# Seven products for eight in the v projection of three layer-1 chunks

## The chip, the cores and the metric

The kernel runs on one core of one Trainium2 chip. The metric is device time in microseconds, the median of several executions of the same program. A core has five engines that run side by side and wait for each other by semaphores: TensorE (matrix products), VectorE and ScalarE (elementwise work), GpSimd (small work and some transfers) and SyncE (which issues most transfers). TensorE writes its results to PSUM, eight banks of 128 x 512 float32; the others copy them from there to SBUF. In the profile they are called PE, DVE, ACT, POOL and SP.

## The reference, cut to what matters

Two layers of attention and gated feed-forward, each with a residual and a normalization in front. The same weights serve both layers.

```python
def _A_ref(x, wqkv, wo):            # x: 1 x 2048 x 1024, wqkv: 1024 x 3072
    qkv = (x @ wqkv) ...            # split into q, k, v of 32 heads of 32
    # token s attends to s, s-2, ..., s-14 (8 keys), softmax, weighted sum of v
    return o @ wo
def _B_ref(x, w1, w3, w2):          # 1024 x 3584, 1024 x 3584, 3584 x 1024
    return (silu(x @ w1) * (x @ w3)) @ w2

x = x + _A_ref(_layernorm(x), A_wqkv, A_wo)
x = x + _B_ref(_layernorm(x), B_w1, B_w3, B_w2)
x = x + _A_ref(_layernorm(x), A_wqkv, A_wo)
x = x + _B_ref(_layernorm(x), B_w1, B_w3, B_w2)
```

The change touches one part: v, the last third of `x @ wqkv`, in the second layer.

## The kernel before

The 2048 tokens are cut in four chunks of 512. The program first computes q, k and v of layer 0 for all four chunks, 24 banks of 8 matmuls for each chunk (for chunk 0, q is done by another routine). Then come eight feed-forward stages, one for each layer and chunk; after the stages 1 to 4 (counted from 0) stands the q, k, v part of one layer-1 chunk. Attention runs on VectorE beside all of this, and its output projection is put in between, two tiles at a time.

From the third stage on, the feed-forward products use a scheme of seven products for eight: the operands are cut in 2 x 2 blocks, sums of blocks are formed, and seven block products (P1 to P7) replace eight. The sums of the weight blocks are made once, during the first two stages, scaled to fit float16, and stored in DRAM (`t_d`); an *early* tile holds the four blocks of P1, P2, P5, P6 and a *late* tile the three of P7, P3, P4. The sums of the activation blocks are four VectorE steps per stage (`norm_sums`), one of them in place.

The plain projection, used for q, k and v alike, writes one bank after the other:

```python
def q_part(l, c, which, ws, then=()):
    ready = ready_norm(("Q", l, c))
    ...
    for t0 in range(0, KT, SG):
        ...                                     # sgt: a slot in big (l = 0) or hT (l = 1)
        for t in range(t0, t0 + SG):
            ps = bank("ps")                     # six PSUM banks in rotation
            for kk in range(KT):
                nc.tensor.matmul(ps[:], lhsT=ws[kk // KH][:, kk % KH, t::KT], rhs=xnT[:, kk, :], ...)
            r = pe(KT, ready)
            background(r)
            nc.scalar.copy(sgt[:, t - t0, :], ps[:])
            ...
        nc.sync.dma_start(qkv_d[l][which][:, t0:t0 + SG, c * CH:(c + 1) * CH], sgt)
        between(False)                          # also puts waiting ScalarE work here
```

The pipeline of seven products works on groups of 256 output rows (two blocks of 128) by 512 tokens; a product is 2 x 4 matmuls of 256 columns. Its steps, cut to what waits for what:

```python
def head_part(i, name):
    if name == "P1":                 # A = P1; B = copy of A
        G["A"] = acc(); run(G, name, G["A"], True)
        G["B"] = acc(); nc.scalar.copy(G["B"][:], G["A"][:])
    elif name == "P5":               # D = P5; s5 = copy of D
        ...
    elif name == "P6":               # A += P6, so after the copy of A; su = copy of A; D += su
        run(G, name, G["A"], False, G["tB"])
        nc.scalar.copy(su, G["A"][:])
        background(t + 0.8)
        nc.vector.tensor_tensor(G["D"][:], G["D"][:], su, op=ALU.add)
    elif name == "P2":               # B += P2: quarter 0 is done
        ...
    elif name == "P7":               # A += P7; s22 = A + s5 on VectorE: quarter 3 is done
        run(G, name, G["A"], False, G["tU"])
        background(r + 0.8)
        if G["corner"]:
            s22 = G["corner"]()
            nc.vector.scalar_tensor_tensor(s22, G["A"][:], G["inv"], s5, op0=ALU.mult, op1=ALU.add)
        ...
    elif name == "P3":               # D += P3: quarter 1 is done
        run(G, name, G["D"], False, G["tD"])
    else:                            # P4: A += P4, after the VectorE step of P7: quarter 2 is done
        run(G, name, G["A"], False, G["tC"])

for i in range(n + 1):               # group i's first half is woven with group i-1's second half
    for name, tail in (("P1", "P7"), ("P5", "P3"), ("P6", "P4"), ("P2", None)):
        if i < n: head_part(i, name)
        if tail and i: head_part(i - 1, tail)
        if tail and i and fill and i == n and tail != "P4": fill(...)
    done(i)
```

(The `fill` puts matmuls of the next product, with w2, between the last P7, P3 and P4; the loop is shortened here.)

ScalarE's and VectorE's work that is not tied to a product waits in queues. The program is put in order when it is built, by clocks (`now`) that the builder keeps for each engine: an item is emitted when these clocks say that it fits. On ScalarE:

```python
gate = [2.2]
def act_background():
    for queue in (acts, sizes, parts, reads):
        while True:
            s = head(queue)
            if s is None or max(now["act"], s[1]) + s[0] > now["pe"] + gate[0]:
                break
            take_act(queue)
```

`acts` are the normalizations: for each half chunk four passes that measure two tiles, a short chain on GpSimd, then two passes that apply (`ACTIVATE xn<-x_sb,mom`), each followed by a DMA transpose to `xnT`. `sizes` measure w2, in squares of 128 x 2048 or 128 x 1536 elements with a sum; `parts` and `reads` measure w1 and w3 and make scaled copies.

The q, k, v part after a stage:

```python
b_stage(u, with_q)
if with_q:
    for which in range(3):
        if which == 2:
            between(False, True)
        q_part(*units[q], which, [weight("qkv"), weight("qkv")])
        release(2)
```

Of the kernel before, what the change touches and what calls it, by code (L numbers as in the profile page):

```python
# [7 lines left out]
FP32 = mybir.dt.float32  # L8
# [9 lines left out]
def kernel(  # L18
# [197 lines left out]
    down_scale = const.tile([P, 2, NG], FP32, name="down_scale")  # L216
    size2 = const.tile([P, 16], FP32, name="size2")
    total = const.tile([P, 1], FP32, name="total")
    down2 = const.tile([P, 1], FP32, name="down2")
    up2 = const.tile([P, 1], FP32, name="up2")  # L220
    peak = const.tile([P, 3], FP32, name="peak")
    hsum = const.tile([P, HTN // 2, HT], FP16, name="hsum")
    h16 = hT[:].bitcast(FP16)
    t2_d = [dram.tile([P, 7, (b - a) // 2, 512], FP16, name=f"t2_d{i}") for i, (a, b) in enumerate(fsplits)]
    t_d = [[dram.tile([P, 14, KT // 2, P], FP16, name=f"t_d{m}_{g}") for g in range(NG)] for m in range(2)]
    qkv_d = [[dram.tile([P, KT, S], BF16, name=f"qkv_d{l}_{i}") for i in range(3)] for l in range(2)]

# [72 lines left out]

    adds, acts, makes, reads, parts, sizes = [], [], [], [], [], []

# [52 lines left out]
    def take_act(queue):  # L355
        cost, ready, emit = queue[0][1]
        act(cost, ready)
        queue[0][1] = None
        emit()
# [3 lines left out]
    def act_background():  # L363
        for queue in (acts, sizes, parts, reads):
            while True:
                s = head(queue)
                if s is None or max(now["act"], s[1]) + s[0] > now["pe"] + gate[0]:
                    break
                take_act(queue)
# [309 lines left out]
    for u in range(len(units)):  # L679
# [14 lines left out]
        if 1 <= u and u + 3 < len(units):  # L694
            seq += [("qkv", which, h) for which in range(3) for h in range(2)]
    w_tiles, w_at, due, used = [], {}, [], [0]

    def load_weight(pieces=1):
# [25 lines left out]
        else:  # L724
# [4 lines left out]
            if rest[0]:  # L729
                got = {}  # L730
                parts.append([weight_size(*rest[0], w, at, got), None])
                reads.append([weight_sums(*rest[0], w, got), None])
        w_at[len(w_tiles)] = at
# [50 lines left out]
    def queue_q(q):  # L784
# [3 lines left out]
        queue_norm(key, units[q][1], range(R))  # L788
        

# [28 lines left out]

    def q_part(l, c, which, ws, then=()):  # L820

# [7 lines left out]
        for t0 in range(0, KT, SG):  # L829
            i = (c * 3 + which) * KT // SG + t0 // SG  # L830
            i = i % (7 if l == 0 else 8) * SG
            sgt = big[:, i * CH:(i + SG) * CH].bitcast(BF16).rearrange("p (a t) -> p a t", a=SG) if l == 0 else hT[:, i:i + SG, :]
# [16 lines left out]
            if l == 0:  # L849
                stored[:] = landed, landed  # L850
            if first and t0 == SG:
# [4 lines left out]
        qkv_at[l, c, which] = landed  # L856
        if which == 1:
            plain_left.discard(("Q", l, c))
        if which == 2:
            xnT_free["Q", l, c] = now["pe"]  # L860
# [54 lines left out]

    pending, stored, made, held = [0] * 2, [0.0] * 2, set(), []
    junk = hsum[:].bitcast(BF16).rearrange("p k t -> p (k t)")

    def differences(m, g, a, r):

        b = blocks[a]
        for out, x, y in ((4, 5, 1), (1, 1, 0), (2, 4, 0), (6, 3, 2)):
            yield 0.40, r, lambda: nc.vector.tensor_tensor(
                b[:, out], b[:, x], b[:, y], op=ALU.add if (x, y) == (4, 0) else ALU.subtract)
        pending[a] -= 1
        nc.gpsimd.dma_start(t_d[m][g][:, 4 * a:4 * (a + 1)], b[:, 0:4])
        nc.gpsimd.dma_start(t_d[m][g][:, 8 + 3 * a:8 + 3 * (a + 1)], b[:, 4:7])
        stored[a] = now["dve"] + 7.0

    def finish_sums(done):  # L930

        while not done():
            if head(reads) is not None:
                take_act(reads)
            elif head(parts) is not None:
                take_act(parts)
            elif head(makes) is not None:
                take(makes)
            else:
                pe_requests(1, True)  # L940
# [60 lines left out]
    def sums_of_w2(i, f, ws, loaded):  # L1001

        while "at" not in got2 or all(pending):
            yield "blocked"
# [30 lines left out]
    def pipeline(key, groups, consume, done, last, fill=None):  # L1035
# [66 lines left out]
        for i in range(n + 1):  # L1102
            for name, tail in (("P1", "P7"), ("P5", "P3"), ("P6", "P4"), ("P2", None)):
# [6 lines left out]
                if tail and i:  # L1110
# [5 lines left out]
                    if fill and i == n and tail != "P4":  # L1116
                        fill(int(tail == "P3"))
            done(i)

    def products(u, f0, f1, hold):  # L1120
# [132 lines left out]
    def b_stage(u, hold):  # L1253
# [5 lines left out]
        for (f0, f1) in fsplits:  # L1259
# [44 lines left out]
            for hh in range(2):  # L1304
                now["pe"] = max(now["pe"], *times[hh])
                for j in range(TPC):
# [10 lines left out]
                    if step == 0:  # L1317
                        steps = range(u * nq // 2, (u + 1) * nq // 2)
                        reads.extend([sums_of_w2(split, f, tiles, max(times[0] + times[1])), None] for f in steps)
                    act_background()  # L1320
# [27 lines left out]
    for c in range(NCH):  # L1348
        for which in range(3):
# [11 lines left out]
            if c >= 1:  # L1361
                then = (then + (None,) * 3)[:3] + (part_of_w2,)
            q_part(0, c, which, w_tiles[2 * which:2 * which + 2], then)
            if c == NCH - 1:
                release(2)
            if which == 0 and c == 1:
# [3 lines left out]
    for u, (l, c) in enumerate(units):  # L1370
# [6 lines left out]
        if with_q:  # L1377
            for which in range(3):
                if which == 2:
                    between(False, True)  # L1380
                q_part(*units[q], which, [weight("qkv"), weight("qkv")])
                release(2)


# [28 lines left out]
```

## Time and profile before

| | |
|---|---|
| time, median of 3 | 1532.38 us (1532.05 to 1533.98) |
| span of the profiled execution | 1531.0 us |
| layer 0: q, k, v of four chunks | to about 192 us |
| feed-forward stages 0 and 1, plain | about 192 to 514 us |
| q, k, v of layer-1 chunk 0 | 514.0 to 556.5 us |
| stages 2, 3, 4, by seven products | from 556.5, 742.8 and 927.1 us |
| q, k, v of layer-1 chunks 1, 2, 3 | 700.9 to 742.8, 885.2 to 927.1, 1072.6 to 1114.1 us |

The span is cut by where the lines of the kernel begin and end on TensorE in the chain that ended last. In the profile a row of groups gives the line, engine, operation, names and shapes, the count, then busy time and mean of one in ns, then idle time before it and what ended it. A row of the timeline gives start and duration in us first. A row of waits gives who waited for whom, the sum in us, the number of times, the longest. A row of the chain in order of time gives start, length and what it was. L836 is the plain projection, L1052 a product of the seven, L1165 one with w2, L840 the eviction of a projection bank, L345 the applying pass of a normalization, L958 a square of w2, L1064 the copy of P1's bank, L1073 that of P6, L1076 VectorE's sum after P6, L1088 and L1090 its sum after P7, L590 and L665 the multiplications of the attention, L771 the output projection.

### The profile page before, as it was taken

How to read it: one execution, taken by the hardware profiler on the slowest of the kernel's cores; microseconds unless marked ns; L12 is line 12 of the kernel's file. 1: busy time of each engine (PE TensorE's matmuls, PEld its weight loads, DVE VectorE, ACT ScalarE, POOL GpSimd, SP SyncE). 2: the span in 40 equal slices, each digit the busy share in tenths (PEclk: the TensorE clock that was granted, in tenths of full speed). 3: DMA queues.
4: the chain of work that ended last, by engine and by line, in shares of the span. 5: the costliest groups of instructions: out<-in, count | busy, mean ns of one | idle time of the engine just before them, and what ended most of it. 6: DMA issues, size and time to landing. Idle time of an engine off the chain costs nothing.

```text
span 1531.0 us, 25095 instructions
## 1 busy us (share of the span) xinstructions
PE 1518.1 (99%) x9594; PEld 989.5 (65%) x9634; DVE 1201.8 (78%) x2126; ACT 884.1 (58%) x1388; POOL 153.7 (10%) x308
## 2 busy tenths in 40 slices
PE   9999999999999999999999999999999999999999
PEld 7666644444444577575786767766677767686865
DVE  4688998889989898989698958898678986435445
ACT  3885476567665357455565564756557445554643
POOL 1210102121211101001011010100111000000000
PEclk9999999999999999999999999999999999999999
DMA  9777969798997888979779997898969988878885
GB/s 321 202 218 215 253 226 330 272 304 289 306 320 247 280 316 294 347 264 303 263 269 324 346 268 282 280 323 302 323 225 333 338 296 282 306 272 334 318 294 203
DMA packets 261432, 439.56 MB, mean 287 GB/s; under 512 B 73856, under 2 KB 201088, under 8 KB 245056
## 3 DMA queue, kind: packets, MB, share of 16 engines
q1 hardware_dynamic: 248464, 390.90, 76.8%
q0 software_dynamic: 12704, 46.93, 8.6%
q8 instruction: 75, 1.23, 0.3%
q14 instruction: 45, 0.37, 0.1%
q10 hardware_dynamic: 144, 0.13, 0.0%
HBM read 345.90 MB, written 67.90 MB: 270 GB/s over the span
## 4 chain that ended last, share of the span: by engine, by line
PE 97%; ACT 1%; issue 1%; DVE 0%; DMA 0%; SPq 0%; ACTq 0%
PE st L1052 32%; PE ps L836 21%; PE w L1165 16%; PE po L771 7%; PE pg L1279 6%; PE pu L1288 6%; PE acc L1310 6%; PE pq L444 1%; PE L L604 0%; DMA wqkv<-in_A_wqkv_dram 0%; ACT L629 0%; ACT L1227 0%; ACT E L629 0%; ACT sg L1227 0%; DVE x_sb L1150 0%
## 5 line engine op out<-in xcount | busy, mean ns | idle before, releaser
L836 PE MATMUL ps<-xnT,wqkv 128*128 128x512 f16 (+1 forms) x1469 | 320.4, 379 | 0.2
L1052 PEld LDWEIGHTS <-early 128*128 128x128 f16 x2688 | 262.6, 98 | 40.4 <-issue 3.5
L836 PEld LDWEIGHTS <-wqkv 128*128 128x128 bf16 x1472 | 210.6, 144 | 108.1 <-issue 2.2
L1165 PE MATMUL w<-t,hT 128*128 128x512 f16 x1008 | 226.0, 379 | 0.6 <-ACT big L1185 0.5
L1052 PEld LDWEIGHTS <-late 128*128 128x128 f16 x2016 | 197.2, 98 | 30.6 <-issue 2.5
L590 DVE TENSOR_TENSOR tree<-qT,kT 128x2048 bf16<-128x2048 bf16 x128 | 156.3, 1221 | 35.8 <-DMA kT<-qkv_d 18.2
L1052 PE MATMUL st<-xnT,late 128*128 128x256 f16 x1344 | 174.2, 273 | 2.2 <-ACT big L1073 2.2
L510 DVE TENSOR_TENSOR tree<-tree 128x1024 bf16<-128x1024 bf16 x256 | 175.6, 686 | 0.9
L1052 PE MATMUL st<-big,early 128*128 128x256 f16 x1344 | 172.3, 273 | 1.6 <-ACT sg L1227 1.1
L1165 PEld LDWEIGHTS <-hT 128*128 128x128 f16 x1008 | 98.2, 98 | 112.9 <-DVE hT L1136 2.0
L1052 PE MATMUL st<-xnT,early 128*128 128x256 f16 x1344 | 165.7, 273 | 0.0
L665 DVE TENSOR_TENSOR tree<-At,vT 128x2048 bf16<-128x2048 bf16 x128 | 156.2, 1221 | 11.9 <-DMA At<-E 10.7
L1064 ACT COPY st<-st 128x512 f32<-128x512 f32 x84 | 48.3, 575 | 128.1 <-PE st L1052 127.4
L771 PE MATMUL po<-wo,oT 128*128 128x512 bf16 x486 | 110.8, 379 | 1.3
L840 ACT CAST hT<-ps 128x512 bf16<-128x512 f32 x96 | 55.8, 585 | 90.6 <-PE ps L836 88.3
L1288 PE MATMUL pu<-xnT,w3t 128*128 128x512 f16 x448 | 105.8, 379 | 0.0
L1279 PE MATMUL pg<-xnT,w1t 128*128 128x512 f16 x448 | 105.8, 379 | 0.0
L1310 PE MATMUL acc<-w2t,hT 128*128 128x512 bf16 x437 | 97.8, 379 | 0.6
L1076 DVE TENSOR_TENSOR st<-st,big 128x512 f32<-128x512 f32 x84 | 58.4, 695 | 46.9 <-ACT big L1073 46.8
L1227 ACT ACTIVATE sg<-st,down_scale 128x512 bf16<-128x512 f32 x126 | 86.6, 687 | 11.6 <-PE st L1052 11.0
L1052 PE MATMUL st<-big,late 128*128 128x256 f16 x672 | 87.1, 273 | 0.0
L771 PEld LDWEIGHTS <-oT 128*128 128x128 bf16 x512 | 50.1, 98 | 55.7
(167 smaller groups left out, 1916.6 us busy)
## 6 DMA issues: line engine op xcount, KB each, us to landing
early<-t_d SPq DMA_DIRECT2D x84, 1024.0 KB, 6.9
late<-t_d SPq DMA_DIRECT2D x84, 768.0 KB, 6.2
t<-t_d SPq DMA_DIRECT2D x42, 1024.0 KB, 7.3
t<-t_d SPq DMA_DIRECT2D x42, 768.0 KB, 5.3
wqkv<-in_A_wqkv_dram SPq DMA_DIRECT2D x28, 1024.0 KB, 8.1
w1t<-in_B_w_dram SPq DMA_DIRECT2D x14, 1024.0 KB, 7.6
w3t<-in_B_w_dram SPq DMA_DIRECT2D x14, 1024.0 KB, 11.0
t_d<-big POOLq DMA_DIRECT2D x28, 512.0 KB, 6.2
```

What stands on the lines that cost most here:

```text
L510: nc.vector.tensor_tensor(b, b, buf[:, 4:8, :], op=ALU.add)
L590: V.tensor_tensor(pr, qT[:], kT[:, :, k0:k0 + TCH], op=ALU.mult)
L665: V.tensor_tensor(tm.rearrange("p w (a e) -> p w a e", a=4), At[:].rearrange("p a w e -> p w a e"), win, op=ALU.mult)
L771: nc.tensor.matmul(ps[:], lhsT=oT[:, t, j * P:(j + 1) * P], rhs=wo[:, t, hh * 512:(hh + 1) * 512], start=(t == 0), stop=(t == KT - 1))
L836: nc.tensor.matmul(ps[:], lhsT=ws[kk // KH][:, kk % KH, t::KT], rhs=xnT[:, kk, :], start=(kk == 0), stop=(kk == KT - 1))
L1052: nc.tensor.matmul(out[:, a, :], lhsT=w[:, a, blk, k, :], rhs=rhs[:, k, :], start=start and a == 0 and k == 0, stop=k == KQ - 1, skip_grou ...
L1076: nc.vector.tensor_tensor(G["D"][:], G["D"][:], su, op=ALU.add)
L1165: nc.tensor.matmul(out[:], lhsT=lhs[:, k, j * P:(j + 1) * P], rhs=w[:, k, :], start=start and k == 0, stop=k == nq - 1, skip_group_check=True)
L1227: nc.scalar.activation(sg[:], src, ACTF.Silu, scale=inv)
L1279: nc.tensor.matmul(pg[:], lhsT=w1t[:, kk, fi * P:(fi + 1) * P], rhs=xnT[:, kk, :], start=(kk == 0), stop=(kk == KT - 1))
L1288: nc.tensor.matmul(pu[:], lhsT=w3t[:, kk, fi * P:(fi + 1) * P], rhs=xnT[:, kk, :], start=(kk == 0), stop=(kk == KT - 1))
L1310: nc.tensor.matmul(acc[:], lhsT=hT[:, f, j * P:(j + 1) * P], rhs=tiles[hh][f // nq][:, f % nq, :], start=(f == 0), stop=(f == f1 - f0 - 1))
```

## The change

Seven products need fewer matmul columns than eight. The change uses them for v of the layer-1 chunks 1, 2 and 3; the q and k parts stay plain. The weights must be scaled and their block sums formed first, so:

- in layer 0, eight ScalarE passes square one eighth of v's weights each and sum the squares. They stand in a queue of their own, `lazy`, behind all the others.
- in the q, k, v part of layer-1 chunk 0 (after stage 1), v is done first, still plain; while v and q run, ScalarE makes 16 scaled copies of v's weight blocks, VectorE 16 differences, and they go to DRAM. The order there is v, q, k.
- for chunks 1, 2 and 3, q and k are plain, and then `v_products` runs a pipeline of two groups. The sums of the activation blocks for it are queued ahead of those for the next stage; the in-place one waits for k.

```diff
     def act_background():
-        for queue in (acts, sizes, parts, reads):
+        for queue in (acts, sizes, parts, reads, lazy):
...
+    def size_of_v(i, w, at):
+
+        for k in range(KH):
+            yield 1.10, at, lambda: nc.scalar.activation(junk[:, 0:D], w[:, k], ACTF.Square,
+                                                         accum_out=size_v[:, KH * i + k:KH * i + k + 1])
+        if i == 1:
+            total_scale(size_v, up_v, down_v, got_v)
+
+    def sums_of_v(ws, at):
...
+                for i, (kh, fh) in ((0, (0, 0)), (1, (0, 1)), (3, (1, 0)), (5, (1, 1))):
+                    t = 4 * g + 2 * fh + a
+                    yield 0.65, max(at, got_v["at"], stored[slot]), lambda: nc.scalar.activation(
+                        b[:, i], ws[kh][:, :, t::KT], ACTF.Copy, scale=up_v[:])
+                makes.append([differences(2, g, a, now["act"] + 0.1, slot), None])
+        made.add("v")
...
     def queue_q(q):
...
         queue_norm(key, units[q][1], range(R))
-        
+        if q > NCH:
+            adds.append([sum_later(key), None])
...
+    def v_products(l, c):
...
+        def consume(G, q, src, r):
+            pair, t0 = q % 2, HT * (q // 2)
+            to = stage(G, pair)
+            if q != 3:
+                nc.scalar.activation(to[:, :, t0:t0 + HT], src, ACTF.Copy, scale=down_v[:])
+                r = act(0.57, r)
...
+        groups = []
+        for g in range(2):
+            G = dict(m=2, g=g, inv=down_v[:])
+            G["corner"] = lambda G=G: stage(G, 1)[:, :, HT:CH]
+            groups.append(G)
+        pipeline(key, groups, consume, lambda i: between(False, i == 0), True)
+        xnT_free[key] = now["pe"]
...
+            if (c, which) == (1, 0):
+                for i in range(2):
+                    lazy.append([size_of_v(i, w_tiles[4 + i], 40.0), None])
             q_part(0, c, which, w_tiles[2 * which:2 * which + 2], then)
             if c == NCH - 1:
+                while which == 2 and head(lazy) is not None:
+                    take_act(lazy)
                 release(2)
...
         if with_q:
-            for which in range(3):
-                if which == 2:
-                    between(False, True)
-                q_part(*units[q], which, [weight("qkv"), weight("qkv")])
+            if u == 1:
+                for which in (2, 0, 1):
...
+                    q_part(*units[q], which, ws, (), 1, 4)
...
+                force(makes, lambda: not any(pending))
+                continue
+            for which in range(2):
+                q_part(*units[q], which, [weight("qkv"), weight("qkv")], (), 1)
                 release(2)
+            v_products(*units[q])
```

The change also orders some queues anew: `finish_sums`, which empties the weight copies at the end of a stage, now lets other VectorE work run in between, and the copies of w2 go ahead of copies of w1 and w3 that are not yet due.

## The prediction

> **What bounds the kernel now.** I read the page's busy shares first, then the chain that ended last, then that chain in order of time, then what TensorE waited for.
>
> ```profile
> PE 1518.1 (99%) x9594; PEld 989.5 (65%) x9634; DVE 1201.8 (78%) x2126; ACT 884.1 (58%) x1388; POOL 153.7 (10%) x308
> PE 97%; ACT 1%; issue 1%; DVE 0%; DMA 0%; SPq 0%; ACTq 0%
> ```
>
> TensorE is the chain: 97% of the span is matmul after matmul. A busy share alone would not prove it; the pace does. From the chain in order of time, one plain stretch and one stretch of seven products:
>
> ```profile
> 700.86 31.08 PE ps L836 x144
> 830.14 34.93 PE st L1052 x320
> ```
>
> 31.08/144 = 0.2158 us for a matmul of 512 columns, 34.93/320 = 0.1092 us for one of 256: nothing stands between them. The longest rows of what TensorE waited for, in the whole kernel:
>
> ```profile
> PE st L1052 <- ACT big L1073: 2.2, 1, 2.2
> PE pq L444 <- DMA wqkv<-in_A_wqkv_dram: 1.4, 2, 0.7
> PE pw L200 <- DVE tree L195: 1.2, 1, 1.2
> PE st L1052 <- ACT sg L1227: 1.1, 1, 1.1
> ...
> ```
>
> So what removes columns gains their full time, and what makes TensorE wait costs its full time. The first row is the only kind of wait that matters below: a product that accumulates onto a bank which ScalarE had not yet copied.
>
> [...] here its 273 ns for 256 columns overlap at a pitch of 109, so I count starts and not durations.
>
> **What is removed.** A plain v part is 8 banks x 8 matmuls x 0.2158 = 13.81 us. Seven products are 2 groups x 7 x 8 = 112 matmuls of 256 columns x 0.1092 = 12.23 us. The difference is 1.58 us, for three chunks 4.75 us, 0.3% of the time. That is the most there is to gain.
>
> **What is added and lies beside.** In layer 0: eight squares of 128x1024, 1.06 us plus 0.2 for the accumulator (the durations of the norms' squares), so 10 us of ScalarE in a stage of 24 banks per chunk, where its busy share is four to eight tenths. In the q, k, v part of the first layer-1 chunk: 16 scaled copies x 0.71 = 11.4 us of ScalarE and 16 differences x 0.42 = 6.8 us of VectorE, in 42 us in which ScalarE was busy for 15; and 3.5 MB of writes. By the order of the compiled program the copies end 12 evictions before this part does. None of it should hold TensorE. Weights for v grow from 2 to 3.5 MB per chunk; six tiles are loaded ahead, so I charge nothing.
>
> **What is added and lies on the path.** The pipeline of seven products has eight or six groups to fill it in the gate and up stages and two here, and after the last group nothing stands between P7, P3 and P4. I walked the three v parts with the durations of the old trace. Zero is the end of k's last bank. A product takes 8 x 0.1092 = 0.873. An engine starts about 0.2 after a product's last slot, as the old trace has it at the first copies of a stage. Rows of the timeline, then of the groups:
>
> ```profile
> 1097.34 1.24 ACT L345 ACTIVATE xn<-x_sb,mom 128x1024 f16<-128x1024 bf16 x1
> 1098.59 0.58 ACT L840 CAST hT<-ps 128x512 bf16<-128x512 f32 x1
> 1099.07 1.24 ACT L345 ACTIVATE xn<-x_sb,mom 128x1024 f16<-128x1024 bf16 x1
> ```
>
> ```profile
> L1088 DVE SCALAR_TENSOR_TENSOR big<-st,down_scale,big 128x512 bf16<-128x512 f32 x42 | 31.4, 748 | 7.8 <-PE st L1052 7.8
> L1076 DVE TENSOR_TENSOR st<-st,big 128x512 f32<-128x512 f32 x84 | 58.4, 695 | 46.9 <-ACT big L1073 46.8
> L665 DVE TENSOR_TENSOR tree<-At,vT 128x2048 bf16<-128x2048 bf16 x128 | 156.2, 1221 | 11.9 <-DMA At<-E 10.7
> ```
>
> *The start.* The first three rows show the norm of the next stage being applied in the shadow of evictions. Before, the plain v part followed them, with six banks of slack. In the compiled changed kernel, in all three chunks, ScalarE's order at the joint is: 15th bank of q and k, apply (1.24), 16th bank, apply, and only then the copy of P1's bank into its second one. The second apply runs from 0.68 to 1.92, the copy to 2.49; P6, third product, accumulates onto the bank being copied and would start at 1.75. It starts at 2.54: 0.8 us lost, three times, 2.4 us.
>
> *The end.* P7's sum is a VectorE step of 0.75 us, and P4 needs it; only P3 (0.87) lies between. 0.2 + 0.75 + 0.05 is 0.13 more than that even with VectorE idle. With the attention steps that stand ahead of it in VectorE's order (a multiplication 1.22, folds 0.69, 0.42 and 0.29) I get, from start to end of v:
> - First of the three chunks: a multiplication, two folds and two of the next stage's sums come between the two P7 sums; P4 starts at 12.9. v takes 13.8 us: nothing gained.
> - Second: VectorE is nearly free. v takes 13.15 us: 0.65 gained.
> - Third: an in-place sum that waits for k's last matmul stands ahead of the value steps, so these start at 0.9; P3 and then P4 wait, P4 starts at 13.85. v takes 14.7 us: 0.9 lost.
>
> Together 41.65 us against 41.45: the 4.75 is given back, 2.4 at the joints and 2.5 at the ends.
>
> *Layer 0.* The eight squares come last among the queues but still move the rest, as the scheduler counts ScalarE's time. In the compiled order the second half of chunk 3's normalization is applied after banks 56 and 60 of the stage; before, after 52 and 53. Chunk 3 starts with bank 65, at 136.5 us. The old run around there:
>
> ```profile
> 122.91 0.58 ACT L840 CAST big<-ps 128x512 bf16<-128x512 f32 x1 [1.14 <-PE ps L836]
> 126.10 1.91 ACT L958 ACTIVATE hsum<-hT 128x2048 bf16<-128x2048 bf16 x1 [2.60 <-DMA hT<-in_B_w_dram]
> 128.14 1.91 ACT L958 ACTIVATE hsum<-hT 128x2048 bf16<-128x2048 bf16 x1
> 130.05 2.03 ACT L840 CAST big<-ps 128x512 bf16<-128x512 f32 x4
> ```
>
> and the landings of the four transposes between 95 and 150 us:
>
> ```profile
> DMA to landing us min/median/max: 4.4/5.0/7.3
> ```
>
> After those four evictions, at 131 to 132, comes the last apply, to 132.3 or 133.3; its transpose lands 4.4 to 7.3 later (last row), at 137 to 138.3 for the median. All 512 columns of every matmul of chunk 3 need it. I expect TensorE to stand there for about 1.4 us.
>
> **The sum.** 1532.4 - 4.75 + 2.4 + 2.5 + 1.4 = 1533.9, with nothing for the rest of the schedule, which is shuffled throughout (attention slips by 10 to 30 us in places, but the last output tile has some 70 us to spare). The old kernel has about 5 us of small gaps in its seven-product stages (stretch less TensorE's busy time, five stages: 1.4, 0.2, 2.9, 0.7, 0.2), and the new one may have more or fewer.
>
> **The rivals.**
> - *The columns win*: the gain stays. For it: the old kernel absorbs the same norms without waiting, and the page shows VectorE at 78%, so many steps may find it free. Against it: slack there came from six banks, and the short pipeline has none. If each v part loses only the 0.13 at its end, and layer 0 nothing: 1532.4 - 4.75 + 0.4 = 1528.
> - *The front decides*: the late transpose costs 4 us or more, as the load of w2 and its squares stand in one queue with it. For it: 7.3 us was seen. Then 1537.
> - *DMA becomes the bound*: 1.5 MB more per chunk and 3.5 MB of writes, where the first q, k, v part already shows 332 GB/s. Against it: the old run holds 300 GB/s through whole stages without a TensorE wait for weights. If the prefetch breaks once per chunk, 2 us each: 1540.
>
> **Range and chances.** The removal is sure to 0.1 us. The joints are 2.4 with an error of 1, the ends 2.5 with 1.5, the front 1.4 with 1.5, the shuffle 0 with 1.5; in squares about 2.8. I say 1533.6, a little below the sum because what a walk by hand sees as waiting is often partly overlapped, with 1530 to 1537. Two per cent is 30 us, and no rival comes near: within 2% 0.985, faster 0.003, slower 0.012.
>
> **What would show it.** TensorE's matmul time should fall by 4.8 us, whatever the end. The list of TensorE's waits should have new rows: for the copy of P1's bank (three times about 0.8), for the VectorE sum of P7 (up to 1.4), and for the transpose in layer 0. The three v parts should take 13.8, 13.2 and 14.7 us, and chunk 3 should start a little late. If these rows are missing and the time is near 1528, the walk is wrong and the pipeline fills better than I think; if the time grows with the v parts at 12.3, the cause lies in the shuffle or the front.

## The result and the profile after

| | before | after |
|---|---|---|
| median | 1533.18 us (1532.05 to 1534.65, 4 runs) | 1558.83 us (1554.53 to 1560.26, 4 runs) |
| span of the profiled execution | 1531.0 us | 1558.5 us |

The change makes the kernel slower: ratio 1.0162, 95% interval 1.014 to 1.0184. The prediction was 1533.6 us with a range to 1537; the time lies 22 us above that range.

The page of the changed kernel, busy shares and chain (for the kernel before these were 1518.1 us and "PE 97%"):

```profile
PE 1527.0 (98%) x9780; PEld 997.6 (64%) x9780; DVE 1223.2 (78%) x2171; ACT 919.3 (59%) x1432; POOL 160.4 (10%) x316
PE 51%; DVE 10%; DMA 5%; ACT 4%; issue 2%; POOL 0%; ACTq 0%; DVEq 0%; POOLq 0%
```

TensorE is no longer a chain of its own: the way back from the end, which the profile follows to 440 us only, now runs through VectorE, DMA and ScalarE too. Its busy time grew by 8.9 us, though it has fewer columns to do, and its idle time (span less busy time) from 12.9 to 31.5 us. What TensorE waited for, after (sum in us, times, longest):

```profile
PE st L1092 <- ACT st L1104: 3.7, 3, 2.6
PE st L1092 <- DVE st L1116: 3.5, 2, 2.8
PE pu L1364 <- DMA w3t<-in_B_w_dram: 3.4, 1, 3.4
PE acc L1386 <- DMA w2t<-in_B_w_dram: 3.3, 2, 2.1
PE ps L844 <- ACT big L848: 3.2, 1, 3.2
PE po L778 <- DVE oT L519: 2.6, 2, 2.3
PE st L1092 <- DMA early<-t_d: 2.2, 1, 2.2
```

Two of these seven rows were predicted: the first (the copy of P1's bank, three times) and the fifth (chunk 3's start in layer 0; the row names an eviction, but only two of the six banks still had one to come, and the transpose that chunk 3 needs landed at 139.15, just before TensorE's start at 139.39). The other five, 15.0 us, are waits of the rest of the schedule: for attention, for weights of the stages 0, 1 and 2, for VectorE's sums.

Why did busy time grow? Windows of the trace after, cut behind three of the waits (columns: window, its length, busy time of each engine with the count, granted TensorE clock, DMA share, GB/s):

```profile
140.10:143.40 3.30, 3.30 (x9) 1.34 (x8) 3.30 (x7) 1.74 (x4) 0.00 (x0) 0.50 0.37 125
...
587.30:590.70 3.40, 3.40 (x19) 2.39 (x18) 3.37 (x5) 1.82 (x4) 0.00 (x0) 0.52 1.07 439
757.90:761.20 3.30, 3.30 (x18) 2.30 (x17) 3.27 (x6) 0.95 (x2) 0.00 (x0) 0.50 1.07 239
```

The clock is at half for 3.4 us behind each of them, and so it is at two other waits (granted 0.51 from 266.4 to 269.8 us and 0.50 from 474.6 to 477.9): five times 3.4 us at half speed, 8.5 us lost. That is most of the 13.7 us by which busy time is above the old one less 4.75. About 2 us more are holes that 40 missing matmul records leave in the old trace (9594 matmuls beside 9634 weight loads; after, none is missing). The rest, some 3 us, I can't assign (the ends of matmuls are modelled, and more waits mean more ends). Before, the trace has no such window inside the kernel (mean granted clock 1.000), not even after its longest stand, of 2.2 us, which ended at 989.79:

```profile
990.00:994.00 4.00, 4.00 (x28) 2.52 (x26) 3.96 (x8) 3.14 (x5) 1.02 (x2) 1.00 1.01 356
```

The length of a wait alone does not tell whether half clock follows. In the trace after, TensorE waited seven times for 2.1 us or more. Behind five of these waits, of 2.1 to 3.4 us, the clock was at half for 3.4 us; the shortest of the five, 2.1 us, ended at 265.87. Behind the other two, of 2.3 and 2.2 us, which ended at 540.95 and 577.78, it stayed full:

```profile
540.90:544.30 3.40, 3.08 (x14) 1.55 (x15) 3.37 (x7) 1.27 (x1) 0.93 (x2) 1.00 1.04 404
577.80:581.20 3.40, 3.40 (x32) 3.04 (x33) 3.33 (x5) 1.75 (x4) 2.18 (x4) 1.00 1.00 413
```

A wait of 2.2 us, as long as the old kernel's longest, was followed by this in one of the kernels below, the one with constant scales and the true cost of the copy:

```profile
1175.13:1178.53 3.40, 3.38 (x13) 1.73 (x13) 3.02 (x6) 2.26 (x3) 1.25 (x3) 0.50 0.99 345
```

The prediction took the clock from the old kernel alone, where it is full throughout, and never priced a wait at its own length plus 1.7 us, the half of those 3.4. What sets the waits with half clock behind them apart from the others was not shown.

Where the 27.5 us lie, from the starts of the stages on TensorE in the two traces:

| part | before, us | after, us | difference |
|---|---|---|---|
| start and layer 0 | 192.5 | 197.1 | +4.6 |
| stage 0 | 161.2 | 166.9 | +5.7 |
| stage 1 and the first layer-1 part together | 202.6 | 213.8 | +11.2 |
| stage 2 | 144.4 | 147.8 | +3.4 |
| second layer-1 part and stage 3 | 184.3 | 188.6 | +4.3 |
| third part and stage 4 | 187.5 | 185.4 | -2.1 |
| fourth part to the end | 458.5 | 458.9 | +0.4 |

So 25 us of the 27.5 come before the first seven-product v part starts at 753 us. The changed v parts, on which the prediction spent most of its work, are a sideshow.

### The profile page after: what moved, and what is told of

It reads as the page before. It is cut to its first block, busy times and chain, and to the rows that moved or that the text cites. A ratio compares the mean times of both kernels' runs of the same rounds, so it can differ in the third digit from the quotient of the medians.

```text
span 1558.5 us, 25594 instructions
## 1 busy us (share of the span) xinstructions
PE 1527.0 (98%) x9780; PEld 997.6 (64%) x9780; DVE 1223.2 (78%) x2171; ACT 919.3 (59%) x1432; POOL 160.4 (10%) x316
## 4 chain that ended last, share of the span: by engine, by line
PE 51%; DVE 10%; DMA 5%; ACT 4%; issue 2%; POOL 0%; ACTq 0%; DVEq 0%; POOLq 0%
PE st L1092 29%; PE w L1241 13%; PE po L778 5%; PE ps L844 4%; DMA t_d<-big 2%; DVE tree L670 2%; DVE tree L515 1%; DVE tree L595 1%; DMA xnT<-xn 1%; DMA w3t<-in_B_w_dram 1%; DMA late<-t_d 1%; DMA At<-E 1%; DVE hT L1212 1%; DVE big L932 1%; DVE tree L517 0%
## 5 line engine op out<-in xcount | busy, mean ns | idle before, releaser
L1092 PEld LDWEIGHTS <-early 128*128 128x128 f16 x2880 | 282.9, 98 | 46.1 <-issue 4.4
L844 PE MATMUL ps<-xnT,wqkv 128*128 128x512 f16 (+1 forms) x1280 | 281.4, 381 | 3.2 <-ACT big L848 3.2
L844 PEld LDWEIGHTS <-wqkv 128*128 128x128 bf16 x1280 | 183.2, 144 | 99.1 <-issue 7.8
L1092 PEld LDWEIGHTS <-late 128*128 128x128 f16 x2160 | 211.3, 98 | 38.4 <-issue 7.3
L1092 PE MATMUL st<-big,early 128*128 128x256 f16 x1440 | 186.3, 274 | 3.7 <-ACT st L1104 3.7
L1092 PE MATMUL st<-xnT,late 128*128 128x256 f16 x1440 | 187.0, 273 | 2.2 <-ACT big L1113 1.1
L1092 PE MATMUL st<-xnT,early 128*128 128x256 f16 x1440 | 177.6, 273 | 2.2 <-DMA early<-t_d 2.2
L778 PE MATMUL po<-wo,oT 128*128 128x512 bf16 x512 | 116.2, 379 | 2.9 <-DVE oT L519 2.6
L1092 PE MATMUL st<-big,late 128*128 128x256 f16 x720 | 93.9, 274 | 3.5 <-DVE st L1116 3.5
L1386 PEld LDWEIGHTS <-hT 128*128 128x128 bf16 x448 | 44.1, 99 | 57.8 <-issue 5.0
## 6 DMA issues: line engine op xcount, KB each, us to landing
w1t<-in_B_w_dram SPq DMA_DIRECT2D x14, 1024.0 KB, 11.4
```

Of the source, the lines that this page charges most:

```text
L778: nc.tensor.matmul(ps[:], lhsT=oT[:, t, j * P:(j + 1) * P], rhs=wo[:, t, hh * 512:(hh + 1) * 512], start=(t == 0), stop=(t == KT - 1))
L1092: nc.tensor.matmul(out[:, a, :], lhsT=w[:, a, blk, k, :], rhs=rhs[:, k, :], start=start and a == 0 and k == 0, stop=k == KQ - 1, skip_grou ...
L1386: nc.tensor.matmul(acc[:], lhsT=hT[:, f, j * P:(j + 1) * P], rhs=tiles[hh][f // nq][:, f % nq, :], start=(f == 0), stop=(f == f1 - f0 - 1))
```

## The experiments

Each time is a median, each ratio is taken against runs of the kernel before on the same chip (1532.1 to 1533.3 us), with its 95% interval. "After" is 1558.83 us. I call the order in which the program is emitted "the order"; the builder makes it from costs it is *told* for each item (`yield cost, ...`), which need not be what the item takes.

**The two queue rules alone**, in the kernel before: `finish_sums` lets VectorE work between, and copies of w2 go ahead.

```diff
-                take(makes)
+                background(head(makes)[1])
+                if head(makes) is not None:
+                    take(makes)
...
-    reads.extend([sums_of_w2(...), None] for f in steps)
+    i = next((i for i, item in enumerate(reads) if item[2] not in held), len(reads))
+    reads[i:i] = [[sums_of_w2(...), None, None] for f in steps]
```

> The kernel before with only the two new queue rules (other VectorE work let in when the copies are finished; copies of w2 ahead of copies not yet due). Theory A: within 2 us of before. Rival B (the rules make the waits of stages 0 and 1): slower by 10 to 20 us.

Measured: 1532.68 us, ratio 1.0001 (0.9992 to 1.0009). The rules cost nothing by themselves, but this shows less than it seems to: in the two traces VectorE, ScalarE, GpSimd and TensorE's weight loads run the same instructions in the same order. In the kernel before, the rules never come into play.

**The squares alone**, in the kernel before: the eight lazy passes and the scale they give, which nothing uses.

```diff
-        for queue in (acts, sizes, parts, reads):
+        for queue in (acts, sizes, parts, reads, lazy):
...
+            if (c, which) == (1, 0):
+                for i in range(2):
+                    lazy.append([size_of_v(i, w_tiles[4 + i], 40.0), None])
```

> The kernel before with the eight squares of v's weights (and the scale made from them) added in layer 0, and nothing else: v stays plain, the scale is not used. Theory A (the squares displace the normalization of chunk 3 and with it the attention and the copies of the first two feed-forward stages): slower than before by 10 to 25 us, with a TensorE wait of 3 to 4 us at chunk 3 and waits in the stages 0 and 1. Rival B (the new queue rules) and rival C (v's block sums and their writes after stage 1): within 4 us of before, for the late transpose alone.

Measured: 1643.16 us, ratio 1.0725 (1.0697 to 1.0753): 111 us for 10 us of ScalarE. VectorE's row of the page (busy tenths in 40 slices), of the kernel before and then of this one:

```profile
DVE  4688998889989898989698958898678986435445
```

```profile
DVE  4778887764544567797979988998959897845445
```

From the eighth slice to the sixteenth (288 to 659 us here) VectorE falls from nearly nine tenths to five: attention, its main work there, is not being emitted. Between 380 and 560 us VectorE adds no output tile, where the old kernel adds eight. What TensorE waited for in this kernel:

```profile
PE po L774 <- DVE oT L517: 25.5, 7, 15.2
PE pg L1292 <- ACT sg L1296: 22.8, 4, 10.1
PE L L607 <- DVE psm L517: 16.5, 1, 16.5
```

The output projection and the scores, put off until the stages could not go on without them, now wait for attention in a row: in the compiled order an output tile that stood 411 us into TensorE's work stands at 525 (in the traces it starts at 413.0 and at 589.5 us). Ten microseconds of filler took a place in the order, and the order collapsed. ScalarE itself was 54% busy.

**The change with the old rules**: as after, without the two rules.

```diff
-                background(head(makes)[1])
-                if head(makes) is not None:
-                    take(makes)
+                take(makes)
```

> The changed kernel with the queue rules of the kernel before. Theory A: no faster than the changed kernel, rather slower (1560 to 1600), as the rules do not make the displacement and may repair a part of it. Rival B: 1538 to 1545. Rival C: within 4 us of the changed kernel.

Measured: 1672.74 us, ratio 1.0915 (1.0893 to 1.0936). So the rules, which change nothing in the old order, are worth 114 us once the squares are there: they let attention back in (between 380 and 560 us the changed kernel again adds eight output tiles, this one none), and what is left of the damage in the changed kernel is a slip of 10 to 30 us.

**The squares later**: queued at chunk 3 of layer 0, where the old kernel has no more to measure.

```diff
-            if (c, which) == (1, 0):
+            if (c, which) == (3, 0):
```

> The changed kernel, with the squares queued at the second part of chunk 3 in place of chunk 1, so after the last normalization of layer 0. Theory A: the waits at chunk 3 and in stages 0 and 1 go, and the time falls from 1559 to 1530 to 1537, what the v parts by themselves cost. Rivals B and C: it stays above 1548.

Measured: 1557.22 us, ratio 1.0167 (1.015 to 1.0184). This missed, and it took away my first explanation. I had thought that the squares stood in front of chunk 3's normalization. That wait does go, but others come in other places:

```profile
PE ps L844 <- DMA wqkv<-in_A_wqkv_dram: 4.8, 2, 3.3
...
PE st L1092 <- DVE st L1116: 3.8, 1, 3.8
```

**No squares**: as after, with constant scales (64 and 1/64) and so without the measurement of v's size.

```diff
+    nc.gpsimd.memset(down_v[:], 1.0 / 64)
+    nc.gpsimd.memset(up_v[:], 64.0)
...
-            if (c, which) == (1, 0):
-                for i in range(2):
-                    lazy.append([size_of_v(i, w_tiles[4 + i], 40.0), None])
```

> The changed kernel without the eight squares: the scale is the constant 64 that they give, everything else stays (block sums made after stage 1, seven products for three chunks). Layer 0 and the stages 0 and 1 are then in the order of the kernel before. Theory A (the squares displace the order, and that is nearly all of the loss): 1529 to 1536. Rival C (making v's block sums and writing them costs as much): above 1542.

Measured: 1539.24 us, ratio 1.004 (1.0026 to 1.0055). 19.6 of the 25.7 us go with the squares. VectorE's instructions now stand in the order of the kernel before up to the first difference for v's sums, at 522 us. About 6 us stay, more than I expected; the next three runs are for these two numbers.

**The squares outside the builder's clocks**: constant scale replaced by the measured one again, with all eight squares put, one each, behind the evictions of chunk 3's q. ScalarE does the same work as in the change, but the builder is not told of it.

```diff
                 r = pe(KT, ready)
                 background(r)
                 nc.scalar.copy(sgt[:, t - t0, :], ps[:])
+                if (l, c, which) == (0, 3, 0):
+                    square_v(t)
+                if (l, c, which, t) == (0, 3, 2, 3):
+                    scale_v()
...
+    def square_v(k):
+        nc.scalar.activation(junk[:, 0:D], w_tiles[4 + k // KH][:, k % KH], ACTF.Square, accum_out=size_v[:, k:k + 1])
```

> The changed kernel with the eight squares done in full, one after each eviction of the q part of chunk 3 in layer 0, and the scale made from them, but without telling the builder's clocks: every other instruction stays in the order of the kernel with the constant scale. Theory A, sharpened (the squares cost by the order that the builder makes of them, not by their 10 us of ScalarE): 1538 to 1542, as with the constant scale. Rival (ScalarE's time itself costs): 1550 or more.

Measured: 1540.4 us, ratio 1.0047 (1.0033 to 1.0061): 1.2 us over the kernel without squares, whose interval it overlaps. So the squares' own time costs about 1 us, within the noise; the other 18 are the order that their told cost makes. Two comparisons rule out the squares' time and their place as the cause. Apart from the squares and their scale, VectorE and ScalarE run the instructions of the kernel with constant scales in the same order to the end. And the run with the squares later put them in the same stretch, 139.8 to 172.4 us against 139.9 to 159.5 here, but told the builder: 1557.22 us. This pair settles the largest part.

**The block sums alone**: as the kernel with constant scales, but v stays plain in all chunks; the sums are made and stored, and nobody reads them.

```diff
-            for which in range(2):
-                q_part(*units[q], which, [weight("qkv"), weight("qkv")], (), 1)
+            for which in range(3):
+                q_part(*units[q], which, [weight("qkv"), weight("qkv")])
                 release(2)
-            v_products(*units[q])
```

> As the kernel without the squares, but v stays plain in all chunks: only the block sums of v are made and stored, and v goes ahead of q and k in the first layer-1 chunk. Theory A: within 3 us of before (1530 to 1536). Rival C: 1542 or more.

Measured: 1540.04 us, ratio 1.0046 (1.0031 to 1.0061): making the sums costs 7 us, with the order v, q, k and the four slots for evictions that come with them. TensorE's longest wait is 4.4 us, of stage 2's P3 for VectorE's `D += su`, and 3.4 us of half clock follow it: most of the 7.

**The seven products alone**: in the kernel before, with the rules, the three v parts by `v_products`. They read block sums of w1 (`t_d += [t_d[0][0:2]]`), so that their v is not v; no squares, no sums of v.

```diff
-            seq += [("qkv", which, h) for which in range(3) for h in range(2)]
+            seq += [("qkv", which, h) for which in ((0, 1, 2) if u == 1 else (0, 1)) for h in range(2)]
+            if u > 1:
+                seq += [("early", 2, 0), ("early", 2, 1), ("late", 2, 0), ("late", 2, 1)]
```

> The seven products alone: no squares, no block sums of v; the products read the stored block sums of w1 instead, so v of three chunks is not v, and the time is that of the products. By the walk in the prediction the v parts cost as much as they save: 1530 to 1536, with TensorE waits of about 0.7 at each joint and 0.1 to 1.4 at each end. If the columns win (the rival): 1527 to 1529.

Measured: 1530.17 us, ratio 0.9984 (0.9977 to 0.9992): 2.9 us faster than its neighbours of the kernel before at the most, 2.5 by the ratio. The products do gain, about half of their 4.75. The page, and the longest wait of TensorE in this kernel:

```profile
PE 1512.6 (99%) x9738; PEld 994.6 (65%) x9778; DVE 1216.5 (80%) x2150; ACT 893.7 (58%) x1400; POOL 155.2 (10%) x310
```

```profile
PE st L1094 <- ACT big L1115: 2.2, 1, 2.2
```

TensorE's busy time is 5.5 us below the old 1518.1 (both traces lack 40 matmul records; here the counts are 9738 and 9778), no half clock, and no wait longer than the 2.2 us of the old kernel. From start to end its v parts take 13.7 (with four matmuls in it that gather attention's scores), 13.46 and 12.36 us, against 13.81 plain and 12.23 of columns.

**The true costs.** The groups of the changed kernel from 500 to 600 us show what a scaled copy of v's weights takes beside a copy of w2's (count, busy us, mean ns):

```profile
L963 ACT ACTIVATE big<-wqkv,up_v 128x512 f16<-128x512 bf16 x8 | 9.9, 1263 | 0.0
L963 ACT ACTIVATE hT<-wqkv,up_v 128x512 f16<-128x512 bf16 x8 | 9.8, 1256 | 2.3 <-DVE tree L595 2.3
L1049 ACT ACTIVATE big<-w2t,up 128x512 f16<-128x512 bf16 x12 | 7.8, 711 | 12.6 <-DMA t_d<-big 11.0 <-issue 1.7
```

Same operation, same shape, same types: 1.26 us against 0.71. The source here, `ws[kh][:, :, t::KT]`, takes every eighth element, that of w2 (`ws[hh][fh][:, f, :]`) is contiguous. No run here changes the stride alone, so that it makes the difference is my guess and not shown. The builder was told 0.65, and I had written 0.71. Two kernels with the cost mended, first the change as it is:

```diff
-            yield 1.10, at, lambda: nc.scalar.activation(junk[:, 0:D], w[:, k], ACTF.Square,
+            yield 1.27, at, lambda: nc.scalar.activation(junk[:, 0:D], w[:, k], ACTF.Square,
...
-                    yield 0.65, max(at, got_v["at"], stored[slot]), lambda: nc.scalar.activation(
+                    yield 1.22, max(at, got_v["at"], stored[slot]), lambda: nc.scalar.activation(
```

> The changed kernel with the builder told the measured durations: 1.27 us for a square (it believed 1.10) and 1.22 for a scaled copy of v's weights (it believed 0.65). If wrong durations in the builder's clocks make the loss, 1530 to 1540. By theory A the squares still displace the layer-0 order, and only the part after stage 1 mends: 1545 to 1556.

Measured: 1547.44 us, ratio 1.0092 (1.0075 to 1.0108), 11 us better than after, still 14 slower than before. True costs help; they don't make the order whole. Against the next kernel, which has the true copies and no squares, the squares still cost 13.5 us.

Then the kernel with constant scales, and only the copy's cost mended (0.65 to 1.22, as above):

> The kernel with the constant scale, with 1.22 us in place of 0.65 for the scaled copy in the builder's clocks. If the 7 us that the block sums cost come from VectorE and ScalarE standing in their order behind copies that take 1.22 us (theory D): 1530 to 1535, and the 5 us wait for the VectorE sum in stage 2 goes. If they come from the copies' time or the writes themselves (rival C): 1537 to 1541, unchanged.

Measured: 1533.92 us, ratio 1.0005 (0.9996 to 1.0013): 5.3 us of the 7 that the sums cost are back. VectorE's waits for the scaled copies, 9.8 us without the mended cost, are gone (4.6 us for another ScalarE step stand in their place), and TensorE's wait for the VectorE sum is halved, not gone as expected. Whether it is the truth of the number or just another order that gives them back, this run does not separate. TensorE's longest row of waits, without and with the mended cost:

```profile
PE st L1094 <- DVE st L1118: 5.0, 2, 4.8
```

```profile
PE st L1094 <- DVE st L1118: 2.2, 1, 2.2
```

The 4.8 us wait, at 569 us, is again stage 2's P3 for `D += su`: VectorE had waited nearly 10 us for ScalarE's slow copies in the part before (rows of 5.4 and 4.4 us), and carried the backlog over.

**A version to beat both**: the last kernel, with the unclocked squares, and P7's last sum put ahead of waiting attention steps.

```diff
-                background(r + 0.8)
+                if (G["m"], i) != (2, 1):
+                    background(r + 0.8)
```

> The last two together with the unclocked squares, and in the last group of a v part nothing of the background ahead of P7's VectorE sum: 1528.5 to 1532, faster than before by 1 to 4 us, if theories A and D hold and the ends of the v parts cost what the prediction said (about 2 us less than with the constant scale and true copies). If not: 1534 or more.

Measured: 1532.56 us, ratio 0.9996 (0.9988 to 1.0004), between the two expectations. It computes all that the change computes, with the true scale, at the time of the kernel before: the same, not faster. The sum put ahead shows no gain: the three v parts take 12.78, 13.07 and 12.36 us with it and without it, and P4 stands for 0.13 us in each. What remains in it, by ScalarE's timeline around 530 us:

```profile
529.46 1.29 ACT L976 ACTIVATE hT<-wqkv,up_v 128x512 f16<-128x512 bf16 x1
535.24 1.07 ACT L848 CAST hT<-ps 128x512 bf16<-128x512 f32 x2 [4.49 <-DMA qkv_d<-hT]
```

ScalarE waits 4.5 us for a store to free a slot; the change leaves four slots for evictions in this part where the old kernel had eight. VectorE waits 4.6 us in turn, P3 of stage 2 waits 2.3, and the clock is at half for 3.4 us behind it.

**Eight slots**: the last kernel, with the block sums of v in the two slots that the other sums use, so that the evictions keep eight.

```diff
-                slot = min((i for i in (1, 2) if not pending[i]), key=lambda i: stored[i])
+                slot = min((i for i in (0, 1) if not pending[i]), key=lambda i: stored[i])
...
-                    q_part(*units[q], which, ws, (), 1, 4)
+                    q_part(*units[q], which, ws, (), 1, 8)
...
+                sums_free[:] = [max(stored[0:2]) + 2.0] * 3
```

> The kernel of the run before it (squares not told to the builder's clocks, scaled copies at their true cost, P7's last sum first; 1532.56 us) with the block sums of v in two of the other tile's slots, so that the evictions of the first layer-1 part have eight slots for stores and not four. Theory C, that what is left there is ScalarE's wait of 4.5 us for stores at 531 us, then VectorE's for ScalarE and a product P3's of 2.3 us with 1.7 us of half clock behind it at 566 us: the three go, 1528.5 to 1530.5 us, faster by 2 to 4. Theory A, that any change of what is told to the builder orders later stages anew and may cost as much as it saves: the wait at 531 us goes, but the time stays within 1531.5 to 1537 us.

Measured: 1544.27 us, ratio 1.0066 (1.0052 to 1.008). Both expectations missed. TensorE's longest row of waits, and then one of VectorE's between 515 and 580 us:

```profile
PE st L1104 <- DVE big L303: 13.2, 2, 8.2
```

```profile
DVE big L303 <- DMA t_dv<-big: 5.7, 2, 5.2
```

The second row is a cost that my edit brought in: the two slots also hold the activation sums of stage 2, which now stand behind the stores of v's sums, and TensorE waits 8.2 us for them at 572 us. (Its other 5.0 us, at 1132 us, lie in a later stage.) And the edit did not do what it was for. ScalarE still waits for a store, now 6.3 us:

```profile
543.28 1.07 ACT L848 CAST hT<-ps 128x512 bf16<-128x512 f32 x2 [6.35 <-DMA qkv_d<-hT]
```

A slot holds two banks and is chosen as `(c * 3 + which) * KT // SG + t0 // SG`, modulo the number of slots. For v (`which` 2) that is 8 to 11 and for q 0 to 3: with the order v, q, k both use the first four of eight, and eight are no more than four. The wait stands at the ninth eviction, q's first. The run therefore says nothing for or against the theory, and what freeing slots by position would be worth stays untried. (The profiled execution took 1552.4 us, 8 above the median, so its trace may hold waits that the others had not.)

## Why the prediction was wrong

By its own steps:

- **What is removed, 4.75 us.** Right as a count of columns. The run with the products alone keeps 2.5 to 2.9 of it. The sign that was given for it, TensorE's busy time lower by 4.8 us whatever the end, did not come: the half clock, which the prediction had nowhere, cost 8.5 us, and busy time rose by 8.9.
- **The start, 0.8 us at each of three joints.** Right in mechanism and, for two of three, in size: P6 waits for the copy of P1's bank 0.72 and 0.72 us at chunks 2 and 3. At chunk 1 it waits 2.7. ScalarE's timeline after, in which P1 starts at 753.23:

```profile
754.32 1.24 ACT L350 ACTIVATE xn<-x_sb,mom 128x1024 f16<-128x1024 bf16 x1 [2.03 <-POOL mom L333]
755.46 0.56 ACT L848 CAST hT<-ps 128x512 bf16<-128x512 f32 x1
755.93 1.24 ACT L350 ACTIVATE xn<-x_sb,mom 128x1024 f16<-128x1024 bf16 x1
757.07 0.58 ACT L1104 COPY st<-st 128x512 f32<-128x512 f32 x1
```

  The order is the one I walked: apply, eviction, apply, copy. But I let the first apply start on time. It waits 2.0 us for GpSimd, everything behind it slides by as much, and the longer wait brings the half clock with it, 1.7 us more. In the kernel with constant scales the wait at chunk 1 is not there at all, and the other two are 0.72 again.
- **The end, v parts of 13.8, 13.15 and 14.7 us.** Measured 16.8, 14.25 and 13.4. The first is 12.23 of columns, 2.73 at the joint, 1.7 of half clock and 0.2 at the end. By the starts of its matmuls, P4 waits 0.18, 0.38 and 0.46 us for P7's sum; the other 0.93 are P3 of chunk 2, which waits for `D += su`. The 0.13 that I had as the least is what P4 waits in all three v parts of the version to beat both. The sum of what is lost at ends is 1.9 us against my 2.5, but the chunks in which it falls are not those I named, because the steps that stand ahead in VectorE's order arrive at other times than in the old trace.
- **Layer 0, 1.4 us.** Right in place, too small: TensorE stands 3.4 us from 136.0 to 139.4, and half clock adds 1.7. The timeline of ScalarE there, after:

```profile
127.58 1.91 ACT L998 ACTIVATE hsum<-hT 128x2048 bf16<-128x2048 bf16 x1 [2.08 <-DMA hT<-in_B_w_dram]
129.62 1.91 ACT L998 ACTIVATE hsum<-hT 128x2048 bf16<-128x2048 bf16 x1
131.53 2.03 ACT L848 CAST big<-ps 128x512 bf16<-128x512 f32 x4
133.43 1.27 ACT L350 ACTIVATE hT<-x_sb,mom 128x1024 f16<-128x1024 bf16 x1
```

  I put the last apply after the four evictions, as here, but at the old trace's 131 to 132. The load of w2 came 1.5 us later than before and so did all behind it; the apply ended at 134.7, the transpose, issued then, landed 4.4 us later, at 139.1.
- **What is added and lies beside: "None of it should hold TensorE."** This step failed. The squares take 1.06 us plus 0.19 as I had it, and put untold beside the evictions they cost about 1 us; but their *told* cost moves the order of everything behind them, and that costs 18 us. The copies were mis-sized: 16 x 1.26 = 20 us, and not 16 x 0.71 = 11.4. Making the block sums costs 7 us.
- **The sum's "nothing for the rest of the schedule".** This is the term that held the result: I set 0 with an error of 1.5, and it was about 18. (The time is 25 us above the sum. The joints took 3.4 of that, half clock included, the front 3.7, and the ends 0.6 less than I had. It is another 18 than that of the squares' order: it has the cost of the block sums in it, and it leaves out the parts of layer 0 and of the joints that the squares' order also moved.) I had seen the warning, that attention slips by 10 to 30 us, and put it aside because the *last* output tile had 70 us to spare. The last tile is the wrong one to look at. SyncE's timeline, before and then after, in stage 0:

```profile
229.42 3.69 SPq L272 DMA_TRANSPOSE xnT<-xn  x2
233.21 14.78 SPq L722 DMA_DIRECT2D w2t<-in_B_w_dram  x4
```

```profile
242.13 4.06 SPq L277 DMA_TRANSPOSE xnT<-xn  x2
246.24 1.30 SPq L552 DMA_DIRECT2D qT<-qkv_d  x1
247.59 0.78 SPq L552 DMA_DIRECT2D kT<-qkv_d  x1
248.47 13.38 SPq L729 DMA_DIRECT2D w2t<-in_B_w_dram  x4
```

  The transposes belong to a norm that waits for output tiles, and these slipped. The loads of w2 stand behind them in SyncE's order and go out 15 us later; they were issued 22.8 us ahead of their use at 256.0, and now 13.4 ahead of it at 261.9. TensorE waits for them 3.3 us in two parts, at 262 and 266. The same at 475 in stage 1: there the loads of w1 and w3 stand behind those of q and k for attention, which waited 19.9 us for VectorE, and go out from 460.1 where they went out from 436.0; TensorE waits 3.4 us for w3. A slip of attention that attention itself can bear is paid by the loads queued behind it.
- **The rivals.** "The columns win", 1528, is nearly what the products alone give, 1530.2. "The front decides" was right about layer 0 alone. "DMA becomes the bound" did not show in its own place: in none of the three v parts does TensorE wait for a load. None of them was a rival of the order as a whole, so the range was built from terms that all had a name, and left out the one that had none.

The ledger: products -2.5 to -2.9, block sums +7 (5.3 of them gone when the copy's told cost is the true one), squares +19.6 (18 of them by order; +13.5 once the costs are true). The items don't add up exactly, to 24 where 25.7 were measured, as each was taken in another order. How the 18 us split among the single slips stays open: each told cost gives another order, and no run undoes one slip alone.

## What to carry to other kernels

When a program is put in order by a cost model at build time, the cost of a "filler" is not its duration but the order that results; compare the compiled positions of the long chains (here attention and the loads behind it in SyncE's order), all of them and not only the last, before pricing the parts. Tell the model the cost of the operation in the form in which it stands, strided source included, and where a small item fits anywhere, put it in by hand without telling the clocks. Price a wait of TensorE of some 2 us or more as one that can bring the half clock behind it (five of the seven waits of 2.1 us or more in the trace after did, at 1.7 us each), and don't take the full clock of one trace for a rule.

## What the runs showed of the hardware that I had not expected

- Half clock of 3.4 us came, in the trace after, behind five of seven waits of TensorE of 2.1 us or more: behind one of 2.1 us, but not behind those of 2.2 and 2.3 us. Of two waits of 2.2 us in two kernels (before; constant scales with the true cost of the copy) one was followed by it and the other was not.
- A ScalarE copy of 128x512 bfloat16 with every eighth element took 1.26 us in the trace after, a contiguous one 0.71.
- The stores of q, k and v (256 KB) land a median of 6.9 us after issue in the first layer-1 part of the kernel before (514 to 575 us), and 10.9 us in the trace after (514 to 575 us), 11.0 and 13.0 us in the last two versions (515 to 570 us), which also write block sums there.
